# Attention with reciprocals widened on ScalarE and turned by four transposes, and with the first two pairs prepared together

## The chip, the cores and the metric

The kernel runs on one core of a Trainium2 chip. The metric is the time of one execution in device microseconds (us), lower is better. The engines are named as in the profile: PE is TensorE's matrix multiply and PEld its weight load, DVE is VectorE, ACT is ScalarE, POOL is GpSimd, SP is SyncE, which here issues most transfers.

## What is computed

Attention over 4 batches, 12 heads, 448 positions and 64 numbers a head, with q and k normalised by their root mean square; then a dense feed-forward layer, and a layer of 8 experts of which each token takes one. Everything is fp32. Cut to what matters here:

```python
def _attn_ref(q, k, v, g_q, g_k):
    def rmsnorm(x, g):
        rms = np.sqrt(np.mean(x * x, axis=-1, keepdims=True) + 1e-06)
        return x / rms * g
    q_n, k_n = (rmsnorm(q, g_q), rmsnorm(k, g_k))
    scores = scale * np.matmul(q_n, k_n.transpose(0, 1, 3, 2))
    scores = scores - np.max(scores, axis=-1, keepdims=True)
    attn = np.exp(scores)
    attn = attn / (np.sum(attn, axis=-1, keepdims=True) + 1e-09)
    return np.matmul(attn, v)

def reference(...):
    x = attention(...)                               # (1792, 768)
    x = leaky_relu(x @ moe_w_in) @ moe_w_out
    return experts(x)                                # gate, w1, relu, w2
```

## The kernel before

Attention goes by pairs of heads of one batch: 24 pairs, in the order of PAIRS (L528). The two heads of a pair stand in the two halves of the 128 partitions. The 448 positions are cut into NC = 4 columns of CP = 112. Products that must be exact are made from a high and a low part (kh, kl, qh, ql), so a score block is three products; a fourth subtracts the row's maximum.

What is done for one pair:

- `load` (L174) fetches q and k (224 KB each), `load_v` v. `square` (L186) squares q and k on ACT and sums each 64 numbers on DVE. `roots` (L203) makes the inverse roots from the sums in nine small DVE instructions, for one pair or for two that `together` (L195) put in one tile. `norm` (L233) multiplies q and k by them, on POOL, but k of the first pair on DVE.
- `turn_k` and `turn_q` (L262, L251) transpose the normalised k and q with four PE transposes each (`turned_of`, L245) into a PSUM tile `tr`, of which there are two. ACT takes the high part from it, DVE the low part; with `apart` the low part of q is made later, where the caller says so. k is also multiplied by the constant `gg`, which `load_constants` (L107) loads and joins on DVE.
- `top` (L271) makes rough scores of a column into the PSUM tile `tp` (one buffer of two banks), and DVE takes their maximum, `md`. `row` (L279) transposes the four maxima into a `tr`, and ACT copies them to `mx`.
- `probs` (L287) makes the exact scores of a column in the PSUM tile `sc` (one buffer of two banks), 8 matmuls, and ACT takes their Exp. `values` (L303) multiplies them with v into the PSUM tile `av`, and POOL adds the columns for the row sums.
- `sums` (L315), `back` (L328): PE adds up the rows and turns the sums around, DVE takes the reciprocals `r`, 112 x 8 numbers. `spread` (L338) writes them to 128 x 448 in a `tr`, with eight matmuls whose stationary side is one column of `r` repeated 64 times and whose moving side is the identity. `scale` (L346) copies that on ACT and multiplies the pair's output by it on DVE. `store` (L352) splits the output into a high and a low part for the layer behind.

`pieces` (L358) holds the order. It prepares pair 0 up to its maxima, then pair 1's norms, and starts the loop over trips i = 0 to 22: in trip i the probabilities and values of pair i (`cur`) run between the tops of pair i + 1 (`one`), the sums and stores of pair i - 1 (`prev`) and the preparation of later pairs. Trips 0 to 2 are written in `begin` (L413), those from FROM = 3 on in `steady` (L456). In trips 8, 10, ... 18 `work` (L805) has one piece of the next layer's weights decoded, five DVE instructions (L581 to L586). Inside this loop the order of instructions on PE, DVE, ACT and POOL is the order in which they are written; the waits are put in by the framework, for every buffer that is used again too. Behind the loop, and for the transfers that SP issues, a planner with a model of the times sets the order: the rest of the attention (ORDER, L530), all other decoding and splitting of weights, and the two layers.

Of the kernel before, what the change touches and what calls it, by code (L numbers as in the profile page):

```python
# [9 lines left out]
F32 = mybir.dt.float32  # L10
# [10 lines left out]
def attention_moe_moe2(  # L21
# [85 lines left out]
    def load_constants():  # L107
        for half in range(2):
            nc.scalar.dma_start(gg[half * DH:(half + 1) * DH, :], g_q.rearrange("(d o) -> d o", o=1))
            nc.scalar.dma_start(gk[half * DH:(half + 1) * DH, :], g_k.rearrange("(d o) -> d o", o=1))  # L110
        nc.vector.scalar_tensor_tensor(gg, gg, ROOT ** -2, gk, ALU.mult, ALU.mult)
# [43 lines left out]
    class Attention:  # L155
# [30 lines left out]
        def square(self, st):  # L186
# [3 lines left out]
            sq = self.early.tile([CP, n, DH], F32, name="sq", bufs=2)  # L190
            for h in (slice(0, n // 2), slice(n // 2, n)) if st is self.first else (slice(0, n),):
                nc.scalar.activation(sq[:, h], flat[:, h], AF.Square, scale=DH ** -0.5)
                nc.vector.tensor_reduce(st["ms"][:, h], sq[:, h], AX.X, ALU.add)
# [39 lines left out]
        def norm(self, st, which=(0, 1)):  # L233
# [5 lines left out]
            for t in which:  # L239
                (nc.vector if t and st is self.first else nc.gpsimd).tensor_tensor(  # L240
# [21 lines left out]
        def turn_k(self, st, i):  # L262
# [5 lines left out]
            nc.vector.scalar_tensor_tensor(kl, tk, gg, kh.bitcast(F32), ALU.mult, ALU.subtract)  # L268
            st.update(kh=kh, kl=kl)

        def top(self, st, c):  # L271

            sc = self.tp()
# [63 lines left out]

        def spread(self, st):  # L338
            tr = st["tr"] = self.tr()
            for c in range(NC):  # L340
                for j in range(2):
                    nc.tensor.matmul(
                        tr[j * DH:(j + 1) * DH, c * CP:(c + 1) * CP],
                        st["r"][:, j, c:c + 1].to_broadcast([CP, DH]), ident[:CP, :CP], start=True, stop=True)
# [13 lines left out]
        def pieces(self):  # L358
# [9 lines left out]
            with tc.manual_schedule(engines={ENG.PE, ENG.DVE, ENG.Activation, ENG.Pool}):  # L368
                fetch(3)
                st = sts[0]  # L370
                self.together(sts[:1])
                self.square(st)
                self.roots(sts[:1])
                self.norm(st)
                self.turn_k(st, 0)
                self.turn_q(st, 0)
                self.together(sts[1:2])
                for c in range(NC):
                    self.top(st, c)
                    if c == 1:  # L380
                        self.square(sts[1])
                self.roots(sts[1:2])
                self.row(st)
                self.norm(sts[1])
# [9 lines left out]
            for op in ORDER:  # L394
                if op == "S":
                    self.sums(sts[n - 2])
                    self.back(sts[n - 2])
                elif op == "C":
# [7 lines left out]
            self.back(last)  # L406
            yield
# [5 lines left out]
        def begin(self, i, sts):  # L413

            cur, one, prev = sts[i], sts[i + 1], sts[i - 1] if i else None
            if i == 0:
                todo = [[("square", 2)], [("roots", 2, 3), ("norm", 2)], [("square", 3)],
                        [("square", 4), ("roots", 3, 5)]]
# [693 lines left out]
```

## Time and profile before

| | |
|---|---|
| runs | 1232.29, 1229.84, 1232.62 us; median 1232.29 |
| profiled execution | 1230.19 us; span from first to last instruction 1228.4 |
| PE busy | 1158.2 us, 94% |
| DVE busy | 775.5 us, 63% |
| ACT busy | 500.3 us, 41% |
| POOL busy | 456.4 us, 37% |
| granted TensorE clock, mean | 0.98 |

The attention takes about the first 345 us; behind it come the dense layer to about 800 us, the routing and the experts. A row of the timeline gives the start in us from the span's start, the time from the start to the end of the last of the instructions merged in it, the engine, the line of the kernel, what is written from what, how many there are, and in brackets the engine's idle time before it and what ended that. Matmuls follow each other in a pipeline, so the time that a group holds PE is the distance from its start to the next group's start, not the duration in its row. A window's row gives the busy time and the number of instructions of each engine, the granted clock of TensorE as a share of full speed, and the share and rate of the DMA engines. In the groups of instructions the numbers behind the first bar are the busy time in us and the mean duration of one in ns, those behind the second the idle time before them.

### The profile page before, as it was taken

How to read it: one execution, taken by the hardware profiler on the slowest of the kernel's cores; microseconds unless marked ns; L12 is line 12 of the kernel's file. 1: busy time of each engine (PE TensorE's matmuls, PEld its weight loads, DVE VectorE, ACT ScalarE, POOL GpSimd, SP SyncE). 2: the span in 40 equal slices, each digit the busy share in tenths (PEclk: the TensorE clock that was granted, in tenths of full speed). 3: DMA queues.
4: the chain of work that ended last, by engine and by line, in shares of the span. 5: the costliest groups of instructions: out<-in, count | busy, mean ns of one | idle time of the engine just before them, and what ended most of it. 6: DMA issues, size and time to landing. Idle time of an engine off the chain costs nothing.

```text
span 1228.4 us, 19094 instructions
## 1 busy us (share of the span) xinstructions
PE 1158.2 (94%) x6988; PEld 930.8 (76%) x6988; DVE 775.5 (63%) x1326; ACT 500.3 (41%) x791; POOL 456.4 (37%) x301
## 2 busy tenths in 40 slices
PE   4899999989899899999999999999799999999997
PEld 2455555545568788888888889888598988998986
DVE  6777888876627786858585854446745179215446
ACT  2566666655335422222222321132344167225444
POOL 1667767757324331313232220000414047113334
PEclk9999999989899999999999999999699999999999
DMA  5212222111102220202020200343357059413456
GB/s 149 60 47 61 68 80 73 50 29 29 46 13 77 78 77 26 78 26 78 26 78 26 78 26 1 133 118 88 117 199 249 24 197 354 153 47 125 172 201 227
DMA packets 68081, 116.28 MB, mean 95 GB/s; under 512 B 6780, under 2 KB 45948, under 8 KB 67968
## 3 DMA queue, kind: packets, MB, share of 16 engines
q1 hardware_dynamic: 64528, 103.87, 26.6%
q0 software_dynamic: 3120, 11.02, 2.6%
q8 instruction: 57, 0.93, 0.3%
q14 instruction: 56, 0.46, 0.1%
q10 hardware_dynamic: 320, 0.00, 0.0%
HBM read 106.61 MB, written 12.58 MB: 97 GB/s over the span
## 4 chain that ended last, share of the span: by engine, by line
PE 77%; DVE 10%; issue 5%; ACT 3%; DMA 2%; POOL 2%; ACTq 0%; DVEq 0%; POOLq 0%; SPq 0%
PE mo L627 6%; PE mo L628 6%; PE mo L629 6%; PE sc L298 6%; PE av L309 6%; PE mp L646 6%; PE mp L647 5%; PE mp L648 5%; PE ph L990 4%; PE ph L989 3%; PE ph L988 3%; PE py L1006 3%; PE py L1004 3%; PE py L1005 3%; DVE w1l L63 2%
## 5 line engine op out<-in xcount | busy, mean ns | idle before, releaser
L654 DVE TENSOR_TENSOR ysum<-mp,ysum 128x448 f32<-128x448 f32 x168 | 103.8, 621 | 111.1 <-PE mp L648 109.5
L313 POOL TENSOR_TENSOR pr<-pr,p 112x896 f32<-112x896 f32 x72 | 153.2, 2128 | 49.6 <-ACT p L300 35.4
L627 PE MATMUL mo<-xTh,w0h 128*128 128x448 f32 x384 | 142.8, 372 | 13.2 <-DVE g L634 9.4
L646 PE MATMUL mp<-gh,w1h 128*128 128x448 f32 x384 | 144.4, 377 | 1.4 <-ACT ysum L652 0.7
L628 PE MATMUL mo<-xTl,w0h 128*128 128x448 f32 x384 | 141.8, 369 | 0.2 <-DVE xTl L63 0.2
L647 PE MATMUL mp<-gl,w1h 128*128 128x448 f32 x384 | 141.8, 369 | 0.0
L629 PE MATMUL mo<-xTh,w0l 128*128 128x448 f32 x384 | 141.4, 368 | 0.0
L648 PE MATMUL mp<-gh,w1l 128*128 128x448 f32 x384 | 140.4, 368 | 0.0
L588 POOL TENSOR_TENSOR raw<-raw,top 128x384 f32<-128x384 f32 x64 | 65.2, 1020 | 191.1 <-DVE raw L586 166.7
L277 DVE TENSOR_REDUCE md<-tp 112x2 f32<-112x896 f32 x96 | 104.4, 1088 | 17.7 <-PE tp L275 17.4
L1004 PE MATMUL py<-w2h,hT 128*128 128x384 f32 x288 | 99.7, 346 | 0.0
L63 POOL TENSOR_TENSOR w1l<-r,w1h 128x1024 fp32r<-128x1024 f32 x17 | 42.9, 2528 | 149.4 <-ACT w1h L952 75.1
L1006 PE MATMUL py<-w2l,hT 128*128 128x384 f32 x288 | 96.8, 336 | 0.0
L1005 PE MATMUL py<-w2h,hL 128*128 128x384 f32 x288 | 96.5, 335 | 0.0
L63 DVE TENSOR_TENSOR hL<-pt,hT 128x512 fp32r<-128x512 f32 x36 | 24.8, 689 | 106.3 <-ACTq L1014 59.3
L627 PEld LDWEIGHTS mo<-xTh,w0h 128*128 128x128 f32 x384 | 72.5, 189 | 24.1 <-DVE g L634 12.1
L990 PE MATMUL ph<-w1l,xgh 128*128 128x512 f32 x216 | 86.4, 400 | 4.2 <-DVE w1l L63 4.2
L988 PE MATMUL ph<-w1h,xgh 128*128 128x512 f32 x216 | 86.7, 402 | 0.0
L989 PE MATMUL ph<-w1h,xgl 128*128 128x512 f32 x216 | 85.8, 397 | 0.0
L63 POOL TENSOR_TENSOR w1l<-raw,w1h 128x768 fp32r<-128x768 f32 x16 | 31.4, 1984 | 141.7 <-ACT w1h L596 141.7
L646 PEld LDWEIGHTS mp<-gh,w1h 128*128 128x128 f32 x384 | 72.4, 189 | 13.0 <-DVE ysum L654 4.1
L300 ACT ACTIVATE p<-sc 112x896 f32<-112x896 f32 x72 | 66.0, 917 | 39.8 <-PE sc L298 35.6
(199 smaller groups left out, 2499.8 us busy)
## 6 DMA issues: line engine op xcount, KB each, us to landing
r<-in_moe_w_dram SPq DMA_DIRECT2D x27, 1024.0 KB, 5.5
r<-in_moe_w_dram SPq DMA_DIRECT2D x36, 768.0 KB, 7.3
wd<-in_moe_w_in_dram SPq DMA_DIRECT2D x32, 384.0 KB, 3.3
wd<-in_moe_w_out_dram SPq DMA_DIRECT2D x32, 384.0 KB, 3.1
qk<-in_q_dram SPq DMA_DIRECT2D x24, 224.0 KB, 3.0
qk<-in_k_dram SPq DMA_DIRECT2D x24, 224.0 KB, 3.2
vv<-in_v_dram SPq DMA_DIRECT2D x24, 224.0 KB, 2.8
x2d<-xn SPq DMA_DIRECT2D x24, 224.0 KB, 2.9
```

The source lines that it names most:

```text
L63: engine.tensor_tensor(dst, src, hi.bitcast(F32), ALU.subtract)
L313: nc.gpsimd.tensor_tensor(st["pr"][:CP], st["pr"][:CP], p, ALU.add)
L627: nc.tensor.matmul(ph, wh_[:, c], xh, start=(c == 0), stop=False)
L628: nc.tensor.matmul(ph, wh_[:, c], xl, start=False, stop=False)
L629: nc.tensor.matmul(ph, wl_[:, c], xh, start=False, stop=(c == KD - 1))
L646: nc.tensor.matmul(py, hi[:, sl], gh, start=(j == 0), stop=False)
L647: nc.tensor.matmul(py, hi[:, sl], gl, start=False, stop=False)
L648: nc.tensor.matmul(py, lo[:, sl], gh, start=False, stop=(j == GF - 1))
L990: nc.tensor.matmul(ph[n], xh[:, c], w1l[:, c, s_], start=False, stop=(c == K1 - 1))
L1004: nc.tensor.matmul(py[n], hT[:, c], w2h[:, c, s_], start=(c == 0), stop=False)
L1005: nc.tensor.matmul(py[n], hL[:, c], w2h[:, c, s_], start=False, stop=False)
L1006: nc.tensor.matmul(py[n], hT[:, c], w2l[:, c, s_], start=False, stop=(c == K2 - 1))
```

## The change

Reciprocals: a new step `widen` has ACT write each reciprocal 64 times to a tile `wide` of 112 x 512, and `spread` turns that tile with the four transposes of `turned_of`. `widen` follows `back` in the order everywhere. `spread` and `scale` move back: in `begin` from the third column to the fourth, behind its top; in `steady` from the third piece to the fourth, behind the top of pair i + 2 and behind `row`, which now stands ahead of `values`. In `steady` the squares of pair i + 6 are made on ACT ahead of `widen`, and summed on DVE where they were.

The beginning: pairs 0 and 1 are squared and their roots made together; the join of the constants stands behind their sums; both norms of pair 0 are made on DVE, those of pair 1 on POOL. Pair 0's tops go to `tp` and `sc` in turn. Pair 1 is turned between them, its low parts behind pair 0's `row`. The roots of pairs 3 and 4 move from the end of trip 0 to the first column of trip 1.

```diff
+
+    def join_constants():
         nc.vector.scalar_tensor_tensor(gg, gg, ROOT ** -2, gk, ALU.mult, ALU.mult)
...
-        def square(self, st):
+        def square(self, st, parts=(0, 1)):
...
             for h in (slice(0, n // 2), slice(n // 2, n)) if st is self.first else (slice(0, n),):
-                nc.scalar.activation(sq[:, h], flat[:, h], AF.Square, scale=DH ** -0.5)
-                nc.vector.tensor_reduce(st["ms"][:, h], sq[:, h], AX.X, ALU.add)
+                if 0 in parts:
+                    nc.scalar.activation(sq[:, h], flat[:, h], AF.Square, scale=DH ** -0.5)
+                if 1 in parts:
+                    nc.vector.tensor_reduce(st["ms"][:, h], sq[:, h], AX.X, ALU.add)
...
-                (nc.vector if t and st is self.first else nc.gpsimd).tensor_tensor(
+                (nc.vector if st is self.first else nc.gpsimd).tensor_tensor(
...
-        def turn_k(self, st, i):
+        def turn_k(self, st, i, apart=False):
...
-            nc.vector.scalar_tensor_tensor(kl, tk, gg, kh.bitcast(F32), ALU.mult, ALU.subtract)
+            st["klow"] = lambda: nc.vector.scalar_tensor_tensor(kl, tk, gg, kh.bitcast(F32), ALU.mult, ALU.subtract)
+            if not apart:
+                st["klow"]()
...
-        def top(self, st, c):
-
-            sc = self.tp()
+        def top(self, st, c, other=0):
+
+            sc = self.sc() if other else self.tp()
...
+        def widen(self, st):
+
+            wide = self.pool.tile([CP, NC, 2, DH], F32, name="wide", bufs=1)
+            nc.scalar.activation(
+                wide, st["r"].rearrange("p j c -> p c j").unsqueeze(3).to_broadcast([CP, NC, 2, DH]), AF.Copy)
+            st["wide"] = wide
+
         def spread(self, st):
-            tr = st["tr"] = self.tr()
-            for c in range(NC):
-                for j in range(2):
-                    nc.tensor.matmul(
-                        tr[j * DH:(j + 1) * DH, c * CP:(c + 1) * CP],
-                        st["r"][:, j, c:c + 1].to_broadcast([CP, DH]), ident[:CP, :CP], start=True, stop=True)
+            st["tr"] = self.turned_of(st["wide"].rearrange("p c j d -> p c (j d)"))
...
-                st = sts[0]
-                self.together(sts[:1])
+                st, one = sts[:2]
+                self.together(sts[:2])
                 self.square(st)
-                self.roots(sts[:1])
-                self.norm(st)
+                self.square(one)
+                join_constants()
+                self.roots(sts[:2])
+                self.norm(st, (1, 0))
+                self.norm(one, (1, 0))
                 self.turn_k(st, 0)
                 self.turn_q(st, 0)
-                self.together(sts[1:2])
                 for c in range(NC):
-                    self.top(st, c)
+                    self.top(st, c, c % 2)
                     if c == 1:
-                        self.square(sts[1])
-                self.roots(sts[1:2])
+                        self.turn_k(one, 1, apart=True)
+                        self.turn_q(one, 1, apart=True)
                 self.row(st)
-                self.norm(sts[1])
+                one["klow"]()
+                one["low"]()
+                self.together(sts[2:3])
...
             if i == 0:
                 todo = [[("square", 2)], [("roots", 2, 3), ("norm", 2)], [("square", 3)],
-                        [("square", 4), ("roots", 3, 5)]]
+                        [("square", 4)]]
             elif i == 1:
-                todo = [[("norm", 3)], [("square", 5)], [("norm", 4)], []]
+                todo = [[("roots", 3, 5), ("norm", 3)], [("square", 5)], [("norm", 4)], []]
...
             for c in range(NC):
-                if c == 3 and prev:
-                    self.scale(prev)
                 self.probs(cur, c)
-                if i == 0 and c == 0:
-                    self.turn_k(one, 1)
-                    self.turn_q(one, 1)
                 self.top(one, c)
                 if c == 2 and prev:
                     self.back(prev)
+                    self.widen(prev)
+                elif c == 3 and prev:
+                    self.spread(prev)
+                    self.scale(prev)
...
-                elif c == 2 and prev:
-                    self.spread(prev)
...
             self.back(prev)
+            if at(i + 6):
+                self.square(at(i + 6), (0,))
+            self.widen(prev)
             self.values(cur, 1)
-            self.spread(prev)
...
             if at(i + 6):
-                self.square(at(i + 6))
+                self.square(at(i + 6), (1,))
             yield
 
-            self.scale(prev)
             self.probs(cur, 3)
             if two:
                 self.top(two, 0)
+            self.row(one)
+            self.spread(prev)
             self.values(cur, 2)
+            self.scale(prev)
             self.store(prev)
-            self.row(one)
```

## Rows read from the trace of the kernel before

**Rows 1.** Windows: trips 0, 1, 2; trips 10, 11 from fourth column to fourth column.

```profile
core 0: us, PE busy (x) PEld busy (x) DVE busy (x) ACT busy (x) POOL busy (x), PEclk, DMA share, GB/s
21.70:39.10 17.40, 14.28 (x75) 7.89 (x74) 11.95 (x26) 9.31 (x12) 7.63 (x6) 1.00 0.20 54
39.10:57.00 17.90, 13.79 (x107) 7.54 (x106) 12.01 (x20) 7.57 (x11) 12.64 (x9) 0.90 0.23 64
57.00:70.20 13.20, 11.99 (x107) 6.78 (x106) 9.61 (x20) 7.56 (x11) 6.32 (x6) 1.00 0.19 54
...
152.20:164.26 12.06, 12.01 (x107) 6.71 (x106) 10.47 (x16) 8.00 (x12) 7.83 (x5) 1.00 0.20 58
164.26:176.00 11.74, 11.74 (x106) 6.72 (x104) 9.29 (x20) 7.56 (x11) 9.74 (x8) 1.00 0.33 94
```

**Rows 2.** Timeline of a steady trip, PE's groups and one Exp.

```profile
163.34 0.99 PE L342 MATMUL tr<-ident,r 112*64 112x112 f32 x16
...
164.26 0.46 PE L298 MATMUL sc<-qh,kh 64*112 64x448 f32 x2
...
165.42 0.92 ACT L300 ACTIVATE p<-sc 112x896 f32<-112x896 f32 x1 [0.44 <-PE sc L298]
...
165.44 0.97 PE L309 MATMUL av<-p,vv 112*64 112x448 f32 x4
...
166.35 0.60 PE L282 MATMUL tr<-ident,md 112*128 112x112 f32 x4
...
166.79 0.55 PE L248 MATMUL tr<-ident,qn 112*128 112x112 f32 x4
...
167.26 0.46 PE L298 MATMUL sc<-qh,kh 64*112 64x448 f32 x2
```

**Rows 3.** Groups of instructions by form, first 560 us.

```profile
L277 DVE TENSOR_REDUCE md<-tp 112x2 f32<-112x896 f32 x96 | 104.4, 1088 | 17.7 <-PE tp L275 17.4
...
L193 DVE TENSOR_REDUCE ms<-sq 112x16 f32<-112x1024 f32 x23 | 28.0, 1218 | 9.9 <-ACT sq L192 9.8
...
L192 ACT ACTIVATE sq<-qk 112x1024 f32<-112x1024 f32 x23 | 24.1, 1050 | 0.0
...
L268 DVE SCALAR_TENSOR_TENSOR kl<-tr,gg,kh 128x448 fp32r<-128x448 f32 x24 | 16.4, 683 | 19.6 <-ACT kh L267 19.6
...
L192 ACT ACTIVATE sq<-qk 112x512 f32<-112x512 f32 x2 | 1.1, 612 | 0.0
```

**Rows 4.** Timeline of the head, all engines.

```profile
8.37 0.17 DVE L213 TENSOR_SCALAR ms<-ms 112x16 f32<-112x16 f32 x1
...
10.24 0.69 DVE L240 TENSOR_TENSOR qn<-qk,y 112x512 f32<-112x512 f32 x1
10.29 1.54 POOL L240 TENSOR_TENSOR qn<-qk,y 112x512 f32<-112x512 f32 x1 [7.44 <-DVE y L222]
...
13.53 0.71 PE L275 MATMUL tp<-kh,qh 64*112 64x448 f32 x2 [0.63 <-ACT qh L256]
...
21.75 0.71 PE L298 MATMUL sc<-qh,kh 64*112 64x448 f32 x2
...
23.63 0.92 ACT L300 ACTIVATE pr<-sc 112x896 f32<-112x896 f32 x1 [1.23 <-PE sc L298]
...
25.24 1.76 PE L248 MATMUL tr<-ident,qn 112*128 112x112 f32 x8 [1.66 <-POOL qn L240]
...
27.63 0.71 PE L275 MATMUL tp<-kh,qh 64*112 64x448 f32 x2 [0.63 <-ACT qh L256]
```

**Rows 5.** DMA issues between 4.1 and 4.2 us; last number: us to landing.

```profile
qk<-in_k_dram SPq DMA_DIRECT2D x1, 224.0 KB, 4.8
```

**Rows 6.** Timeline, all engines, end of trip 0 and start of trip 1.

```profile
39.85 2.08 DVE L214 TENSOR_SCALAR y<-ms 112x32 int32<-112x32 int32 x1
...
45.69 0.45 PE L275 MATMUL tp<-kh,qh 64*112 64x448 f32 x2 [3.42 <-DVE md L277]
```

**Rows 7.** Timeline of PE, a stall in trip 18.

```profile
262.72 1.76 PE L342 MATMUL tr<-ident,r 112*64 112x112 f32 x16 [3.97 <-DVE r L335]
```

**Rows 8.** Timeline of DVE, the same stall.

```profile
261.12 1.42 DVE L582 SCALAR_TENSOR_TENSOR top<-wd,top 128x384 int32<-128x384 int32 x1
```

More of the change, by code (lines that the diff above doesn't have):

```diff
@@ L184, in load_v @@
                 st["v"], v[b, 2 * hp:2 * hp + 2].rearrange("h (p c) d -> p h (c d)", c=NC))
-        def square(self, st):
+        def square(self, st, parts=(0, 1)):
             n = 4 * NC
             flat = st["qk"].rearrange("p t h (c d) -> p (t h c) d", d=DH)
-            sq = self.early.tile([CP, n, DH], F32, name="sq", bufs=2)
+            if 0 in parts:
+                st["sq"] = self.early.tile([CP, n, DH], F32, name="sq", bufs=2)
+            sq = st["sq"]
             for h in (slice(0, n // 2), slice(n // 2, n)) if st is self.first else (slice(0, n),):
-                nc.scalar.activation(sq[:, h], flat[:, h], AF.Square, scale=DH ** -0.5)
-                nc.vector.tensor_reduce(st["ms"][:, h], sq[:, h], AX.X, ALU.add)
+                if 0 in parts:
+                    nc.scalar.activation(sq[:, h], flat[:, h], AF.Square, scale=DH ** -0.5)
+                if 1 in parts:
+                    nc.vector.tensor_reduce(st["ms"][:, h], sq[:, h], AX.X, ALU.add)
         def together(self, sts):
@@ L397, in pieces @@
                     self.back(sts[n - 2])
+                    self.widen(sts[n - 2])
                 elif op == "C":
@@ L406, in pieces @@
             self.back(last)
+            self.widen(last)
             yield
@@ L417, in begin @@
                 todo = [[("square", 2)], [("roots", 2, 3), ("norm", 2)], [("square", 3)],
-                        [("square", 4), ("roots", 3, 5)]]
+                        [("square", 4)]]
             elif i == 1:
-                todo = [[("norm", 3)], [("square", 5)], [("norm", 4)], []]
+                todo = [[("roots", 3, 5), ("norm", 3)], [("square", 5)], [("norm", 4)], []]
             else:
                 todo = [[("square", 6)], [("roots", 5, 7), ("norm", 5)], [("norm", 6)], []]
-            for lo, hi in {0: ((2, 3), (3, 5)), 1: ((5, 7),)}.get(i, ()):
+            for lo, hi in {0: ((3, 5),), 1: ((5, 7),)}.get(i, ()):
                 self.together(sts[lo:hi])
             for c in range(NC):
-                if c == 3 and prev:
-                    self.scale(prev)
                 self.probs(cur, c)
-                if i == 0 and c == 0:
-                    self.turn_k(one, 1)
-                    self.turn_q(one, 1)
                 self.top(one, c)
```

## The prediction, made before the change was run

> **What bounds the kernel now.** I read the page first: its busy line puts TensorE (PE) far ahead, but a share of the whole span hides stages. So next come the windows, one for each trip of the attention loop. There the reader is to see two kinds of trip. In a steady one PE is busy in all of 11.74 us; VectorE (DVE) has 9.3 us of work in it and ScalarE (ACT) 7.6 [rows 1]. There only less work on PE makes it shorter. A trip in which DVE also decodes a piece of weights takes 12.06 us, with DVE at 10.5: there DVE is near the bound too [rows 1]. The first trips are different: 17.4, 17.9 and 13.2 us, with PE idle for 3.1 us of the first and 4.1 of the second [rows 1]. Third, the timeline of a steady trip gives the price of each group of matmuls, as the distance from its start to the next group's [rows 2]. Fourth, the timeline of the head, and of two stalls, says who waits there [rows 4, 6 to 8]. The clock is read from the pitch of equal matmuls, for the granted clock reads 1.00 in the first trip [rows 1] though its eight transposes at 25.24 us hold PE for 1.76 us [rows 4], and eight in a steady trip for 0.91 (166.35 to 167.26) [rows 2]: the lower level (1.2 GHz) against the upper (2.4).
>
> **Part 1: spread as transposes.** Removed for each pair are 8 fp32 matmuls (16 instructions), which hold PE for 164.26 - 163.34 = 0.92 us [rows 2]. Added are 4 transposes of 112 columns. The kernel makes such groups already: four take 0.44 us (row) and 0.47 (turn_k) [rows 2]. I take 0.47, so a gain of 0.45 us a pair.
> The widening on ACT writes 112x512 numbers; an ACTIVATE of that size took 0.61 us, one of twice the size 1.05 [rows 3]; these are the bounds, and I take 0.61. ACT is busy for 8.0 of 12.06 us, so it fits beside PE [rows 1]. It waits for the reciprocal, and behind it on ACT stand the Exp of the fourth column and row's copy. The Exp starts 1.16 us after that column's matmuls (164.26 to 165.42) [rows 2], so the cover holds unless the reciprocal is over a microsecond late; then each microsecond more is paid by PE. Widening sits between reciprocal and transposes, but the transposes now come after the fourth column's matmuls, one top and row: 1.18 (164.26 to 165.44) + 0.44 = 1.6 us later on PE [rows 2]. So its 0.6 us is hidden and the reciprocal gets 1 us of slack that it didn't have.
> In return scale, store and kl of a later pair come about 1 us later against PE, and the next top's maximum on DVE behind them. In a plain trip the slack covers that. In a trip with decoding it may not: DVE has 10.5 us of work for a period of 12.06 - 0.45 = 11.6 [rows 1]. I bound the gain there by -0.3 (the 0.3 by which that trip is longer than the plain one comes once more) and 0.45 and take 0.15, in between, since both engines are near their bound. The split of square moves only ACT's half ahead of the widening; its reduction stays in place: nothing.
>
> **Part 2: the head.** Pair 1 is now squared before pair 0's roots. Its k is issued between 4.1 and 4.2 us and lands 4.8 us later, at 8.9 [rows 5]. Its square takes 1.05 us and the reduction 1.22 [rows 3]: 11.2. Then come the joined constant and the roots, 1.87 us for one pair (8.37 to 10.24) [rows 4], some 2.2 for both with twice the width: pair 0's norms start at 13.4 instead of 10.24. From there to the first top went 3.3 us, with POOL's half of the norm (1.54) as the later one; both on DVE at 0.69 each end 0.15 us sooner [rows 4]. First top: 16.5, 3.0 us later than before.
> The tops now alternate between two PSUM buffers, so DVE reduces without waiting for PE. The first result after 0.7 us, four reductions of 1.09 less a little overlap, a gap of 0.4 for the turns of pair 1, kl of pair 1 (0.68, which row must await, because row writes the buffer that kl reads) [rows 3] and row at the head's pitch (0.88, half of 1.76) make 6.9 us where the first top to the first probabilities took 8.2 [rows 4]. First probabilities: 23.4, 1.7 us later than 21.75.
> Then the payback. Before, PE waited until 25.24 for pair 1's norm on POOL, turned it, and made pair 1's first top at 27.63, with the second column of pair 0 right behind [rows 4]. Now pair 1 is ready, and the second column awaits only the Exp of the first, which ended 2.8 us after the matmuls began (21.75 to 23.63, and 0.92) [rows 4]: 26.2. That is 1.6 us sooner than 27.8.
> The roots of pairs 3 and 4 leave the end of the first trip. There one of their instructions, 32 numbers wide, took 2.08 us while POOL was adding, and PE stood 3.42 us for a top [rows 6], after which its clock fell (0.90 granted over the trip [rows 1]). In their new place, behind the second trip's first top, they are again beside POOL's additions, but two tops and four groups lie between them and the next waiting top: I take a wait of 1.5. So the second trip takes 11.7 (a steady one) + 1.5 = 13.2 instead of 17.9: 4.7 gained, bounds 2 and 6. The third, whose PE idles for 1.2 of 13.2 us [rows 1], loses most of that and 0.45: 1.3. The fourth gains 0.4. The head: 1.6 + 4.7 + 1.3 + 0.4 = 8.0 us, bounds 4 and 11.
>
> **Part 3: the rest.** Of the 14 trips from the fifth, 9 are plain (9 x 0.45 = 4.05) and 5 decode (5 x 0.15 = 0.75). The last five would give 2.25. In one of them the reciprocal sat behind a decoding step on DVE [rows 8]; PE waited 3.97 us for it and went on at the lower level, 1.76 us for the spread [rows 7]. With 1.6 us of PE's work now ahead of the spread, 1.8 of that go. The last two pairs run among expert matmuls, PE bound: 0.9. Together 9.75.
> Sum: 8.0 + 9.75 = 17.75 us. The profiled execution took 1230.2, so 1212.4. The median of the runs is 2.1 above it, and the sum isn't good to that; I say 1212.
>
> **A rule that speaks against it.** Eight transposes already stand in a row in each steady trip, at the upper level's pitch, and the granted clock of these trips is 1.00 [rows 1, 2]. The Trainium skill (TensorE: Matmul & The Clock Gate, Part 4: PE-mode transpose) says that one transpose took about 275 ns in a kernel, and that transposes don't engage the fast clock. By its price, as an estimate, four cost 1.1 us, and 24 pairs would lose 4.3 us to the 0.92 of now where the sum gains; the trace shows less than half of that price.
>
> **The rivals.** (a) DVE takes over: the later kl and the maxima behind it hold up tops, in plain trips too, and nothing is left of the 4.8 us in the 14 trips and the 4.05 in the last five. For: 12.06 against 11.74 [rows 1]. Against: the plain trip has the roots in it, and PE shows no gap. Time: 1212.4 + 8.85 = 1221.
> (b) More comes back: the spread's slack removes the whole stall [rows 7] with its slow stretch (3 to 5 us more), and PE reaches the upper level earlier in the head (2 to 4 us more). For: the reciprocal no longer stands directly ahead of PE. Against: the decoding step still delays the maximum that a top needs. 1205.
> (c) Transposes are dear: with twelve to a trip the clock falls for them. At the pitch of the head, four take 0.88 us [rows 4] instead of 0.92, and the 9.3 us that the sum counts for spreads (3 x 0.45 in the head, 4.05, 0.75, 2.25 and 0.9) are gone; if the fall takes the next group along, some 4 us more. Against: the pitch of eight in a row [rows 2]. 1212.4 + 9.3 + 4 = 1226. This is where the skill's rule on the clock, named above, would lead.
> (d) Slower: decoding steps that the written order doesn't fix fall to new places. One of a step's instructions took 1.42 us beside POOL's work [rows 8], and the step cost PE 4 us of waiting and then the half pitch, 0.8 in the spread alone, for which I take 2.5 in all [rows 7]. Each more like it costs 6.5 us; with three more the gain is gone, with four it is 1212.4 + 26 = 1238, slower. For: the stall stands in the trace, and the planner sees other times. Against: the decoding trip of 12.06 us has PE busy for 12.01 [rows 1].
> (e) It does less than it says: pair 1 still isn't ready in time, or one or two such collisions take the head's gain: 1229.
>
> **How the numbers follow.** Forecast 0.57; (a) 0.17, (b) 0.12, (c) 0.03, (d) 0.05, (e) 0.06. A measurement tells 0.3%, 3.7 us, from no change. Faster are the forecast, (a), (b) and (c): 0.89. Same is (e): 0.06. Slower is (d): 0.05. The range takes the bounds of the head (-3 and +4) and of the trips, and reaches over most of (b) and (a) to (c): 1203 to 1226.
>
> **What would show it.** Steady trips of 11.3 to 11.4 us with four transposes in 0.44 to 0.48; first probabilities near 23.4 and the second trip begun some 1.6 us sooner; the steady trips begun 8 us sooner; no wait of PE for the reciprocal. Wrong it would be if tops wait for maxima in plain trips, if the widening holds up an Exp, or if a new stall of 4 us or more stands after 250 us.

## The result and the profile after

The changed kernel takes 1214.25 us (median of four runs, 1213.58 to 1214.98) where the kernel before takes 1232.39 beside it: a ratio of 0.986, 95% interval 0.984 to 0.9875. The forecast was 1212. The profiled execution took 1213.58 us, with a span of 1211.9; the profiled execution of before took 1230.2, so in the two traces the gain is 16.6 us where the sum had 17.75.

The page's busy line comes first, that of before above that of the changed kernel. TensorE (PE) has 288 instructions fewer (6988 before) and 12.6 us less to do (1158.2 before), so some 4 us of the gain are idle time that went; the 12.6 hold removed work and slow stretches.

```profile
PE 1158.2 (94%) x6988; PEld 930.8 (76%) x6988; DVE 775.5 (63%) x1326; ACT 500.3 (41%) x791; POOL 456.4 (37%) x301
...
PE 1145.6 (95%) x6700; PEld 920.2 (76%) x6700; DVE 776.5 (64%) x1318; ACT 510.0 (42%) x815; POOL 455.2 (38%) x300
```

The windows answer [rows 1]: the first three trips, then a decoding and a plain steady trip.

```profile
core 0: us, PE busy (x) PEld busy (x) DVE busy (x) ACT busy (x) POOL busy (x), PEclk, DMA share, GB/s
24.30:37.60 13.30, 11.82 (x65) 6.18 (x64) 9.24 (x17) 8.13 (x10) 5.17 (x4) 1.00 0.13 36
37.60:50.30 12.70, 11.81 (x93) 6.36 (x92) 10.44 (x20) 7.87 (x12) 10.70 (x8) 1.00 0.20 61
50.30:62.88 12.58, 11.65 (x93) 6.34 (x92) 9.70 (x20) 8.02 (x12) 8.01 (x7) 1.00 0.29 86
142.20:153.97 11.77, 11.62 (x94) 6.35 (x92) 10.11 (x15) 8.93 (x14) 8.17 (x6) 1.00 0.21 61
153.97:165.39 11.42, 11.42 (x95) 6.37 (x94) 9.59 (x19) 7.60 (x13) 9.43 (x7) 1.00 0.29 95
```

The second trip fell from 17.9 to 12.7 us and no longer shows a granted clock of 0.90. The plain trip is 0.32 us shorter, with PE still busy in all of it. The decoding trip is 0.29 us shorter, and PE now has 0.15 us of idle time in it.

The timeline of PE in a steady trip answers [rows 2]. From start to start, row takes 0.44 us, the spread by four transposes 0.48, and the transposes of a later pair's k, now directly behind values, 0.53.

```profile
155.18 0.60 PE L290 MATMUL tr<-ident,md 112*128 112x112 f32 x4
155.62 0.55 PE L254 MATMUL tr<-ident,wide 112*128 112x112 f32 x4
156.10 0.97 PE L317 MATMUL av<-p,vv 112*64 112x448 f32 x4
157.00 0.60 PE L254 MATMUL tr<-ident,qn 112*128 112x112 f32 x4
```

The head, from the timelines of VectorE (DVE), GpSimd (POOL) and PE, answers [rows 4].

```profile
13.29 2.14 DVE L246 TENSOR_TENSOR qn<-qk,y 112x512 f32<-112x512 f32 x2
...
13.34 2.99 POOL L246 TENSOR_TENSOR qn<-qk,y 112x512 f32<-112x512 f32 x2 [10.49 <-DVE y L228]
...
17.13 0.72 PE L283 MATMUL tp<-kh,qh 64*112 64x448 f32 x2 [0.63 <-ACT qh L262]
...
23.42 0.98 PE L290 MATMUL tr<-ident,md 112*128 112x112 f32 x4 [2.50 <-DVE kl L274]
24.33 0.71 PE L306 MATMUL sc<-qh,kh 64*112 64x448 f32 x2
...
27.18 0.72 PE L306 MATMUL sc<-qh,kh 64*112 64x448 f32 x2 [0.64 <-ACT pr L308]
```

Two norms on DVE take 2.14 us while POOL runs its two (2.99). The row of before that priced one at 0.69 had POOL's beside it too, begun 0.05 us later [rows 4]; here the first of the two also takes 0.69, and the second, begun while POOL is at work, 1.53. The row waits for the late part of pair 1's k.

Two stalls near the end, in the 19th and the 22nd trip, answer [rows 7, 8]. PE first, then DVE and the queue of ScalarE (ACT) in the second of them.

```profile
249.28 0.45 PE L283 MATMUL tp<-kh,qh 64*112 64x448 f32 x2 [1.50 <-DVE md L285]
...
251.41 0.60 PE L254 MATMUL tr<-ident,wide 112*128 112x112 f32 x4 [1.15 <-ACT wide L349]
...
290.26 1.01 PE L254 MATMUL tr<-ident,wide 112*128 112x112 f32 x4 [2.39 <-ACT wide L349]
```

```profile
286.75 0.19 DVE L343 RECIPROCAL r<-av 112x8 f32<-112x8 f32 x1
...
289.14 0.55 ACT L596 ACTIVATE mag<-wd 128x384 f32<-128x384 f32 x1 [3.74 <-DMA wd<-in_moe_w_out_dram]
289.60 0.61 ACT L349 ACTIVATE wide<-r 112x512 f32<-112x512 f32 x1
```

The 19th trip's wait for the reciprocal (3.97 us before) is now 1.15 us for the widened tile, after 1.50 for a maximum. The 22nd trip has a new stall: the reciprocal was done at 286.94, but the widening stood in ACT's queue behind a decode that waited for its weights.

### The profile page after: what moved, and what is told of

The parts are those of the page before. It is cut to its first block, busy times and chain, and to the rows that moved or that the text cites. A ratio compares the mean times of both kernels' runs of the same rounds, so it can differ in the third digit from the quotient of the medians.

```text
span 1211.9 us, 18550 instructions
## 1 busy us (share of the span) xinstructions
PE 1145.6 (95%) x6700; PEld 920.2 (76%) x6700; DVE 776.5 (64%) x1318; ACT 510.0 (42%) x815; POOL 455.2 (38%) x300
## 4 chain that ended last, share of the span: by engine, by line
PE 71%; DVE 15%; issue 4%; ACT 4%; DMA 3%; POOL 2%; ACTq 0%; DVEq 0%; SPq 0%; POOLq 0%
PE mo L643 6%; PE mo L644 6%; PE mo L645 6%; PE sc L306 5%; PE mp L662 5%; PE mp L663 5%; PE mp L664 5%; PE av L317 5%; PE ph L1006 4%; PE ph L1005 3%; PE ph L1004 3%; PE py L1022 3%; PE py L1020 3%; PE py L1021 3%; DVE w1l L63 3%
```

## The experiments

All kernels can be laid side by side by one mark: the start of the Exp of a trip's first column, of which each trace has 24. Selected marks in us, with the median time and the ratio to runs of the kernel before on the same chip (there its medians are 1231.49 to 1232.39):

```
trip                 1st    2nd    3rd    5th    6th   19th   20th   22nd   23rd | median   ratio, 95% interval
before             23.63  40.20  58.07  85.39  97.16 251.66 270.32 293.87 308.16 | 1232.39
after              26.21  38.71  51.41  78.52  89.47 239.58 255.97 278.81 294.77 | 1214.25  0.986  0.984-0.9875
e1_spread_only     24.19  40.29  60.86  87.97  98.91 249.05 265.51 288.30 302.99 | 1223.95  0.9935 0.992-0.995
e2_head_only       26.03  38.85  52.31  79.64  91.42 245.90 264.89 288.44 302.73 | 1226.88  0.997  0.9955-0.998
e3_place_only      26.09  38.68  51.52  78.59  89.91 245.20 262.42 286.16 302.45 | 1225.10  0.995  0.994-0.997
e4_old_place       25.88  38.23  53.46  83.02  95.45 260.21 278.29 302.51 321.49 | 1241.74  1.009  1.007-1.010
e5_roots_back      26.46  38.95  59.28  86.38  97.33 247.44 264.52 288.24 303.38 | 1221.70  0.990  0.988-0.993
e6_one_bank        28.01  40.57  53.27  80.37  91.30 241.37 256.47 279.07 294.81 | 1217.54  0.9885 0.987-0.990
e7_widen_dve       26.34  38.69  51.86  80.02  90.95 241.22 261.24 284.69 300.46 | 1218.66  0.989  0.987-0.990
e8_head_tuned      22.59  35.02  47.77  74.79  85.72 235.78 252.13 275.00 290.88 | 1210.34  0.982  0.981-0.984
e9_decode_behind   22.82  35.37  48.08  75.11  86.03 236.11 253.13 276.26 291.85 | 1214.06  0.986  0.985-0.988
e11_roots_only     23.58  39.65  53.09  80.44  92.19 246.72 265.54 289.09 303.37 | 1225.89  0.996  0.9945-0.997
```

**The new spread without the new head.** The kernel before with the widening, the four transposes and their new places, and in steady trips the squares on ACT ahead of the widening:

```diff
-            tr = st["tr"] = self.tr()
-            ... (eight matmuls of r by ident)
+            st["tr"] = self.turned_of(st["wide"].rearrange("p c j d -> p c (j d)"))
...
     self.back(prev)
+    self.widen(prev)
```

> The kernel before with one part of the change: the reciprocals are widened on ScalarE, turned by four transposes, and the spread, the scaling and the row stand at their new places; the head with the first two pairs is the old one. Theory A (two savings that add): each of the 24 trips gives back 0.38 us by the four transposes (1.83 to 1.45 us of TensorE time), 9.1 us together, give or take 2 for stalls that move; the head gives nothing, so the first probabilities stay at about 21.8 us and the fourth trip ends where it did but for some 1.5 us of transposes. Time 1223 us. Rival B (the new places and the stalls that they end do the work, the head is nearly all later taken back): 1217 us or less. Rival C (all of the gain is the head; the eight matmuls were hidden in waits): within 3 us of 1232.

Measured: 1223.95 us, 8.2 less than before beside it, near theory A's 1223, but not by its terms alone. From the sixth trip's mark to the 19th's (13 steady trips) it takes 150.14 us where before takes 154.50 and the changed kernel 150.11: 0.34 us a trip. The 19th trip gives 2.2 more (16.46 us from mark to mark instead of 18.66). But the second trip became longer, 20.57 us instead of 17.87, which theory A didn't have; the roots stall is still there and costs more in this trace (below, with the roots moved back).

**The new head without the new spread.** The changed kernel with the eight matmuls at their old places:

> The kernel with the change, but the reciprocals are spread by the eight matmuls at their old places, with no widening: the new head alone. Theory A: the head's trips give back what the two traces show less the transposes' share in trips 1 to 3, about 7 us, and nothing of it is lost later: 1225 us; the first probabilities at 24.3 us, the fifth trip starting about 7 us sooner than in the kernel before, steady trips as long as before (12.06 and 11.74 us). Rival B: the later trips meet transfers or ScalarE's decode sooner, and the dense layer takes part of it back: 1229 us or more. Rival C: all of the gain is the head: 1215 us.

Measured: 1226.88 us, 5.3 less than before. At the fifth trip's mark 5.75 us are gained; the 13 steady trips then take 154.48 us, as before, and the 19th trip keeps its full wait of 3.97 us for the reciprocal. Theory A holds with 5.3 to 5.8 us in place of 7. The two parts alone make 8.2 + 5.3 = 13.5 us of the 18.1: by the medians they don't simply add. In the traces the first matmul of the dense layer comes 5.9 us sooner with the spread alone, 5.5 with the head alone and 16.6 with both, so 5.2 are missing there. At the fifth trip's mark the spread alone is 2.58 us late, the head alone 5.75 early, and both together 6.87 early: 3.7 of the missing are there, in the long second trip of the spread alone.

**The new places with the old matmuls.** The changed kernel, no widening, eight matmuls where the transposes stand:

> The kernel with the change, but with the eight matmuls in place of the widening and the four transposes, at the new places. Theory A (the matmuls' price, 0.92 against 0.44 us): steady trips 0.4 us longer than with the transposes, 24 of them 9 to 10 us, less up to 2 us because ScalarE's widening no longer stands behind the decode's wait in the trip that starts at 277.7 us: 1222 us. Rival B (the place does it: the reciprocal is never waited for at the new place, whatever spreads it): within 3 us of the changed kernel, 1214 to 1217 us.

Measured: 1225.10 us, 10.9 more than the changed kernel. The 13 steady trips take 155.29 us: 0.40 us a trip more than with transposes, and 0.06 more than before the change. So in steady trips the whole gain is the price of the four transposes, and the new place by itself gives nothing there. It gives something in the 19th trip, from mark to mark 17.22 us (18.66 before, 16.39 in the changed kernel). Of the 10.4 us between the two profiled executions 5.6 are there at the 19th trip's mark; the rest comes behind it and is not taken apart here.

**The transposes at the old place.** The changed kernel, with the spread directly behind the second column's values:

```diff
     self.widen(prev)
     self.values(cur, 1)
+    self.spread(prev)
...
     self.row(one)
-    self.spread(prev)
     self.values(cur, 2)
```

> The kernel with the change, the widening and the transposes kept, but the transposes at the old place, directly behind the second column's values, and the row behind the third column's values again. Theory A: the chain from the column matmuls (reciprocal 0.2 us, ScalarE 0.6 us) no longer lies under the fourth column's probabilities, TensorE waits 0.4 to 0.8 us for the widened tile in each of some 20 trips, which takes 8 to 16 us: 1222 to 1230 us, with the widening named in TensorE's list of waits. Rival B (ScalarE is free at once and the second column's values cover the chain): under 0.1 us in a trip, 1214 to 1217 us.

Measured: 1241.74 us, slower than the kernel before, and by more than either theory had. PE's list of waits from 100 to 330 us, and one trip in the timelines of PE, ACT and DVE:

```profile
PE tr L254 <- ACT wide L349: 21.2, 17, 4.6
```

```profile
152.50 0.97 PE L317 MATMUL av<-p,vv 112*64 112x448 f32 x4
154.69 0.60 PE L254 MATMUL tr<-ident,wide 112*128 112x112 f32 x4 [1.22 <-ACT wide L349]
...
153.07 1.05 ACT L197 ACTIVATE sq<-qk 112x1024 f32<-112x1024 f32 x1
154.02 0.62 ACT L349 ACTIVATE wide<-r 112x512 f32<-112x512 f32 x1
...
153.13 0.20 DVE L343 RECIPROCAL r<-av 112x8 f32<-112x8 f32 x1
```

The reciprocal is ready at 153.33. The widening starts at 154.02, because the squares of a later pair stand ahead of it on ACT (0.69 us), and takes 0.62; PE waits 1.22. That is the longest such wait of the 13 steady trips; in the others it is 0.64 to 0.94. These trips take 164.76 us, 1.13 a trip more than in the changed kernel: 0.85 are the waits, and most of the rest lies in two trips of 14.0 us in place of 12.4, the 8th and the 12th. The window of the 8th shows why:

```profile
120.29:134.25 13.96, 13.02 (x94) 6.87 (x92) 9.59 (x20) 8.07 (x13) 9.46 (x7) 0.88 0.18 51
```

The granted clock is 0.88 there, 1.00 in the trip before it. Part of the waits belongs to the squares, which the change put ahead of the widening and which stayed there. Without them, as an estimate from the rows of this trip (1.22 - 0.69), PE would still wait 0.53 us, more than the 0.40 that the transposes save; no run shows that order. In this kernel, then, the new place is what makes the transposes pay: without 1.6 us of other work on PE ahead of them they cost more than the matmuls did.

**The roots of pairs 3 and 4 moved back.** The changed kernel with one line at its old place:

```diff
-                        [("square", 4)]]
+                        [("square", 4), ("roots", 3, 5)]]
...
-                todo = [[("roots", 3, 5), ("norm", 3)], ...
+                todo = [[("norm", 3)], ...
```

> The changed kernel with one line moved back: the roots of pairs 3 and 4 are taken at the end of the first trip again, not at the beginning of the second. Theory A (the stall of the kernel before in its second trip came from the roots standing on VectorE ahead of the next column's maximum): the second trip, 12.7 us from its probabilities to the next trip's in the changed kernel, is 3 to 4 us longer, TensorE waits there for a maximum, and 3 of them are still there in the fifth trip: 1217 us. Rival B (that trip was long because the second pair had to be prepared in it, and the roots are hidden now): under 1 us in that trip, 1214 to 1215 us.

Measured: 1221.70 us, 7.4 more than the changed kernel. The second trip takes 20.33 us from mark to mark instead of 12.70: the stall of theory A, at twice its price in this execution. The timelines of POOL, DVE and PE, and the windows behind the stall:

```profile
34.60 6.48 POOL L321 TENSOR_TENSOR pr<-pr,p 112x896 f32<-112x896 f32 x3
...
37.46 1.45 DVE L219 TENSOR_SCALAR ms<-ms 112x32 f32<-112x32 f32 x1
38.94 0.18 DVE L220 TENSOR_SCALAR y<-ms 112x32 int32<-112x32 int32 x1
39.16 1.98 DVE L222 TENSOR_TENSOR a<-y 112x32 f32<-112x32 f32 x1
...
44.68 0.71 PE L283 MATMUL tp<-kh,qh 64*112 64x448 f32 x2 [3.66 <-DVE md L285]
```

```profile
46.00:50.00 4.00, 4.00 (x30) 1.93 (x26) 1.13 (x2) 1.44 (x3) 2.76 (x2) 0.50 0.33 106
50.00:54.00 4.00, 4.00 (x18) 2.33 (x18) 1.73 (x3) 1.41 (x2) 3.37 (x3) 0.50 0.38 107
```

Two root instructions of 0.18 and 0.19 us take 1.45 and 1.98 beside POOL's additions, the maximum behind them comes late, and PE stands for 3.66 us. Then it works at the lower level (granted clock 0.50) for over 8 us. In the profiled execution of the kernel before, after a wait of 3.42, it was back at 1.00 by the window from 50 to 54 us:

```profile
46.00:50.00 4.00, 4.00 (x32) 2.12 (x30) 1.37 (x2) 1.30 (x2) 2.43 (x2) 0.57 0.65 172
50.00:54.00 4.00, 3.56 (x38) 2.23 (x34) 2.33 (x4) 1.46 (x2) 3.71 (x3) 1.00 0.31 86
```

With waits so much alike, it is the longer slow stretch that makes the stall cost 7.6 us in this trace and 4.4 in that one; the trace of the new spread alone also shows 0.50 up to 54 us and 0.72 in the four behind. But the four executions with the roots moved back took 1222.22, 1217.92, 1221.99 and 1221.41 us, the shortest at a mean granted clock of 0.982 and the others at 0.977, and the one in the trace is the longest. The shortest is 3.7 us above the median of the changed kernel. So the price of 7.6 us is that of this execution, and not shown to be that of the kernel.

**Only the roots moved, in the kernel before.** The reverse of that edit:

> The kernel before with one line moved: the roots of pairs 3 and 4 are taken at the beginning of the second trip in place of the end of the first, as in the changed kernel; the second pair is still prepared inside the first trip, and the reciprocals are spread by the eight matmuls. Theory A (of the head's gain the roots are the greater part and preparing two pairs together the smaller, as moving the roots back cost 7.4 us where the new head without the new spread gained 5.3): the second trip is 3.5 to 4.5 us shorter than its 17.9 us, the fifth trip starts 3.5 to 4.5 us sooner, and the time is 1228 us. Rival B (with the second pair prepared in the first trip the stall only moves to the roots' new place): under 1 us, 1231 to 1232 us.

Measured: 1225.89 us, 5.6 less than before: as much as the whole new head without the new spread (5.3). The second trip takes 13.44 us instead of 17.87, and at the fifth trip's mark 4.95 us are gained where the whole head gains 5.75. DVE and PE at the roots' new place:

```profile
40.86 1.05 DVE L213 TENSOR_SCALAR ms<-ms 112x32 f32<-112x32 f32 x1
42.02 0.18 DVE L214 TENSOR_SCALAR y<-ms 112x32 int32<-112x32 int32 x1
...
43.70 1.08 DVE L277 TENSOR_REDUCE md<-tp 112x2 f32<-112x896 f32 x1
...
44.84 0.45 PE L275 MATMUL tp<-kh,qh 64*112 64x448 f32 x2 [0.50 <-DVE md L277]
```

One instruction is stretched, not two, and PE waits 0.50 us. Theory A holds for the trip (4.4), and the time is 2 us better than its 1228. Preparing two pairs together adds 0.8 us to this (against the head alone), or 1.6 (the new spread alone against the kernel with the roots moved back, at the fifth trip's mark).

**One bank for the first tops.**

```diff
-                    self.top(st, c, c % 2)
+                    self.top(st, c)
```

> The changed kernel, but the four tops of the first pair all go through the one bank of the kernel before, so each waits until the maximum of the one ahead of it has been read. Theory A: the second and the fourth top each start about 0.7 to 1.0 us later, and the first probabilities come 1.0 to 1.8 us after the 24.3 us of the changed kernel: 1215.5 us if it stays. Rival B (the transposes of the second pair and the late part of its k set the row, not the banks): under 0.4 us.

Measured: the first Exp comes 1.80 us later, and 1.79 of it are still there at the 19th trip; the profiled execution is 2.1 us longer, the median (1217.54) 3.3. Theory A, at its upper end. What the head loses ahead of the steady trips is kept by them.

**The widening on DVE.**

```diff
-            nc.scalar.activation(
-                wide, st["r"]..., AF.Copy)
+            nc.vector.tensor_copy(
+                wide, st["r"]...)
```

> The changed kernel with the widening on VectorE, directly behind the reciprocal, in place of ScalarE. Theory A (in the trip that starts at 277.7 us ScalarE's decode, which waits for its weights to land, stands ahead of the widening; the reciprocal itself was in time): TensorE's waits of 1.2 and 2.4 us for the widened tile in the 19th and 22nd trip are gone, and the half clock behind the second; steady plain trips stay at 11.4 us, decode trips are up to 0.3 us longer, for VectorE's 0.6 us more. 1211 us, of which 3 us in the 22nd trip. Rival B (VectorE is the next bound and its maxima come later in each trip): decode trips 0.5 us longer and more, 1217 us or more.

Measured: 1218.66 us, 4.4 more. Steady trips stay (150.27 us for the 13). The wait for the widened tile in the 22nd trip falls from 2.39 us to 0.26, as theory A has it, but waits for Exps come behind it, of 0.86 us in this trip and 1.93 at the start of the next (15.77 us for the trip, 15.96 in the changed kernel), and the 19th trip takes 20.02 us instead of 16.39. There, DVE and PE:

```profile
252.13 0.20 DVE L343 RECIPROCAL r<-av 112x8 f32<-112x8 f32 x1
252.31 2.24 DVE L599 SCALAR_TENSOR_TENSOR top<-mag,top 128x384 f32<-128x384 f32 x1
254.48 1.26 DVE L349 COPY wide<-r 112x512 f32<-112x512 f32 x1
...
255.79 1.01 PE L254 MATMUL tr<-ident,wide 112*128 112x112 f32 x4 [3.89 <-DVE wide L349]
```

On DVE a decode step gets between reciprocal and widening, and beside POOL it takes 2.24 us instead of 0.56. Neither theory had that: the cause in the 22nd trip was named rightly, but taking the widening to the other queue only changes which decode step stands in its way.

**A tuned head.** Three edits to the changed kernel: v of the first pair is loaded behind pair 1's q and k, pair 1 is normalised on DVE too, and its kl is made ahead of the third maximum.

```diff
-    att.load_v(att.first)
...
+                fetch(2)
+                self.load_v(self.first)
                 fetch(3)
...
-                (nc.vector if st is self.first else nc.gpsimd).tensor_tensor(
+                (nc.vector if vec else nc.gpsimd).tensor_tensor(
...
-                        self.turn_k(one, 1, apart=True)
+                        self.turn_k(one, 1)
```

> The changed kernel with three edits in the head: the first values are loaded behind the second pair's q and k; the second pair is normalised on VectorE as the first is, not on GpSimd beside it; the late part of the second pair's k is taken ahead of the third maximum. Theory A (each of the three was in the chain to the first probabilities): the squares of the second pair's k start at about 7.7 in place of 8.9 us; the first pair's two norms take 1.4 in place of 2.1 us; the row starts when the fourth maximum ends and not 0.6 us later; together the first probabilities come at about 22 us in place of 24.3 and the time is 1212 us. Rival B (the first values or a later load then come too late, or VectorE is the bound of the head and the norms only change their queue): the first probabilities at 23.5 us or later, 1214 us.

Measured: 1210.34 us (1209.79 to 1211.68), below all runs of the changed kernel. ACT, DVE and PE:

```profile
7.17 1.06 ACT L197 ACTIVATE sq<-qk 112x1024 f32<-112x1024 f32 x1 [0.99 <-DMA qk<-in_k_dram]
...
11.53 2.50 DVE L246 TENSOR_TENSOR qn<-qk,y 112x512 f32<-112x512 f32 x4
...
17.49 0.68 DVE L274 SCALAR_TENSOR_TENSOR kl<-tr,gg,kh 128x448 fp32r<-128x448 f32 x1
...
20.72 0.71 PE L306 MATMUL sc<-qh,kh 64*112 64x448 f32 x2
```

Pair 1's k is squared 1.77 us sooner, four norms on DVE alone take 2.50 us (two had taken 2.14 beside POOL), and the first probabilities start at 20.72 instead of 24.33: 3.6 us where 2.3 were expected. The three edits were not run one by one. At the 19th trip the gain is 3.8, and in the median 3.9.

**The late decodes put behind.** The tuned head, with the decode of the seventh and the eighth weight half queued behind the widening on ACT and behind the reciprocal, or the next maximum, on DVE:

```diff
+                with tc.issue_after(behind["a"].ins) if behind else ExitStack():
                     nc.scalar.activation(mag, hi.bitcast(F32), AF.Abs)
+                with tc.issue_after(behind["v"].ins) if behind else ExitStack():
                     nc.vector.tensor_scalar(top, hi, 3, 0x3FFFFFF8, ...)
```

> The kernel of the tuned head with two edits of order: the decode of the seventh weight half (in the 19th trip) and of the eighth (in the 22nd), which both wait for a transfer, are queued behind that trip's widening on ScalarE and, on VectorE, the seventh behind that trip's reciprocal and the eighth behind the next pair's first maximum. Theory A (the two late transfers reach TensorE only through the work queued behind the decode): the waits of 1.5 and 1.2 us in the 19th trip and of 2.3 us in the 22nd, with the half clock behind them, are gone; the 19th trip takes about 14 us in place of 16.4 and the 22nd 13 in place of 15.9; 1206 us. Rival B (the weights are then late for the first units of the dense layer, or VectorE's decode meets other maxima): the start of the dense layer gains under 1 us, 1210 us.

Measured: 1214.06 us, 3.7 more than the tuned head. The waits for the widened tile go, but DVE and PE in the 19th trip show a new one:

```profile
242.97 0.20 DVE L343 RECIPROCAL r<-av 112x8 f32<-112x8 f32 x1
243.74 1.01 DVE L606 TENSOR_SCALAR top<-wd 128x384 int32<-128x384 int32 x1 [0.57 <-DMA wd<-in_moe_w_out_dram]
244.79 2.33 DVE L607 SCALAR_TENSOR_TENSOR top<-wd,top 128x384 int32<-128x384 int32 x1
247.22 2.26 DVE L608 SCALAR_TENSOR_TENSOR top<-mag,top 128x384 f32<-128x384 f32 x1
...
251.66 0.46 PE L283 MATMUL tp<-kh,qh 64*112 64x448 f32 x2 [3.80 <-DVE md L285]
```

The decode steps now meet two additions of POOL, which ran from 244.49 to 249.07, and are stretched to 2.3 us each; the maximum behind them is late, and PE waits 3.80. Theory A falls: the transfer wasn't the only cause; the decode's place against POOL's additions is one too. In the 22nd trip and at the start of the 23rd two waits for Exps (1.17 and 2.80 us) replace the one for the widened tile. About 2 us more are lost behind the 24th trip's mark; of these the runs don't show the cause.

## Why the prediction was right, point by point

**The sum.** 17.75 us were forecast between the two profiled executions, 16.6 measured: 1212.4 against 1213.58. The forecast was then rounded down by 0.4, and the median stands 0.7 us above the profiled execution; that makes up the distance from 1212 to 1214.25. Several terms were off by more than this, and their errors cancel.

**The four transposes.** Priced at 0.47 us, they take 0.48; the matmuls' 0.92 is confirmed by the experiment that puts them back (0.40 us a trip). The term was a little too large in plain trips (0.45 forecast; 0.32 in the windows shown, some 0.38 between the marks), because the next transposes, moved behind values, take 0.53 instead of 0.47. In decoding trips it was too small (0.15 forecast; 0.29 in the windows, some 0.26 between the marks): the maxima do come later, and PE is idle for 0.15 us, but the rest of the gain stays. Over the 13 steady trips, 8 plain and 5 decoding, 4.39 us are gained, where the forecast's rates make 8 x 0.45 + 5 x 0.15 = 4.35: the two errors cancel, which is luck. Rival (a) didn't come: from the fourth trip to the end of attention tops wait 2.7 us for maxima, 1.5 of it in the stall at 249 us.

The Trainium skill (TensorE: Matmul & The Clock Gate, Part 4: PE-mode transpose) gives about 275 ns for one transpose in one kernel and says that transposes don't engage the fast clock. For these fp32 transposes in a stream of other matmuls the trace shows another price: four stand at a pitch of 0.12 us, and with sixteen to a trip (rival (c) counted twelve, which is the number before) the granted clock is 1.00 in the steady trips' windows. What transposes alone would do to the clock no run here shows. Rival (c), where that rule led, is out.

**The hidden widening.** Right, and for the reason given. It takes 0.61 to 0.63 us on ACT, and PE waits for it in none of the 13 steady trips; it does in the second trip (0.11 us), the third (0.37), the 19th, the 22nd and the last (0.96). With the transposes at the old place it is waited for in all of the 13, for 0.85 us on average. The forecast had counted the slack and its price ("each microsecond more is paid by PE"); that is what the old place pays.

**The head.** By the starts of the first probabilities the fifth trip begins 7.95 us sooner (8.0 forecast), by the Exps 6.87, since in that trip the store now stands ahead of an Exp on ACT, of which 0.50 us reach PE. Term by term: the second trip starts 1.49 us sooner (1.6), and is 5.17 shorter (4.7); the third gives 0.63 (1.3) and the fourth 0.66 (0.4). That these add up to 8.0 is partly luck. The wait of 1.5 us taken for the roots' new place was 0.29 (for the top at 43.70). In the third trip PE keeps 0.93 us of idle time of its 1.2, where most was to go. And the second column, which the sum put at 27.8 before and 26.2 after, started at 28.14 and 27.18: only 0.96 of the 1.49 us come from there. The first top came at 17.13 (16.5), for a term that was mis-sized: two norms at 0.69 on DVE were priced from a row in which DVE had started 0.05 us ahead of POOL [rows 4], and took 2.14 us together. The first probabilities at 24.33 (23.4) carry that on. That the roots were the larger part is shown by moving them alone (4.95 of 5.75 us), and the pricing of the two together at 1.6 by the two pairs of runs that differ in it (0.8 and 1.6).

**What was missed** is that the roots' stall has no one price. The sum took 4.7 us from the trace of the kernel before. In the two other traces that still have the stall, with nearly the same wait, the second trip takes 20.3 and 20.6 us instead of 17.9, with over 8 us at the lower level. The sum is not hurt by it, because the changed kernel doesn't have the stall. It does bear on whether the two parts add: the trace of the spread alone is such a long one, and of its four executions (1221.96 to 1225.44 us) the longest. Whether the longer slow stretch comes with the shorter trips, or with one execution and not another of the same kernel, is not settled here, and so it isn't shown that each part is worth more beside the other.

**The last trips.** 4.95 us were forecast for all behind the 18th trip, and about 4.5 came, but not as told. The 19th trip gave 2.3 (2.25 forecast). The 22nd lost 1.7: "no wait of PE for the reciprocal" was wrong, since the widening made ACT's queue a part of that chain, and a decode waiting for weights stood in it. That is a small case of rival (d): one collision at 1.7 us, not 6.5. From the 23rd trip's mark to the dense layer's first matmul (304.8 us, 321.4 before) another 3.2 us were gained; there the kernel before had two waits for maxima, of 2.2 and 1.9 us, and the changed kernel has one of 1.2. The planner ordered the two differently (the 23rd trip's last column stands ahead of that matmul only in the changed kernel), so the 3.2 are not the price of one thing.

## What to carry to other kernels

Price a replacement by the pitch of the same form where the kernel already runs it, and then ask what the new producer chain needs: the four transposes were worth 0.4 us a trip with 1.6 us of other work put ahead of them, and with the same instructions at the old place, behind the squares on ScalarE, the kernel took 9.5 us more than before. When a change bundles several edits, look for the one line: moving nine small VectorE instructions, the roots, away from GpSimd's additions and from the next maximum gave as much as the whole rebuilt head without the new spread. Try a head that is wholly on the critical path first, since what was gained there (3.6 us in the tuned head) was there in the end (3.9), whereas waits near the end came back in another queue each time one was removed.

## What the runs showed of the hardware

Small VectorE instructions on SBUF tiles are stretched, by up to eleven times, while GpSimd adds: 0.18 us to 2.08 for a root step [rows 6], 0.19 to 1.98 for another, 0.54 to 2.33 for a decode step. Two norms took 2.14 beside GpSimd's, where four with GpSimd idle took 2.50. The maxima, which read PSUM, stayed at 1.08 to 1.09 us in all of these stretches. The Trainium skill (SBUF — State Buffer, Who interferes with whom) says that a VectorE instruction with two inputs in SBUF contends with a GpSimd instruction that reads there, that one in a mode of two ports contends with GpSimd, and that a reduction doesn't. The rows agree, and they show the order of the price: a stretched root step ends 0.03 to 0.05 us after the addition of some 2.1 us beside it, a decode step 0.4 after. A root step that began 0.01 us ahead of an addition (38.94 against 38.95, with the roots moved back) kept its 0.18 us.

In the traces the same stall of 3.4 to 3.9 us was followed by some 3 us at the lower clock level in one kernel and by over 8 in two others, one execution of each.
